# Five of nine small tiles one place earlier, and three routing groups regrouped and re-timed, in an attention and expert kernel

## The chip, the cores and the metric

The kernel runs on one core of one Trainium2 chip. The metric is the device time of one launch in microseconds (us). Three runs of the kernel before gave 518.86, 519.31 and 521.41 us; their median is 519.31 us.

A core has a matrix engine (TensorE, PE in the profile), a vector engine (VectorE, DVE), a scalar engine (ScalarE, ACT), a general engine (GpSimd, POOL) and a sync engine (SyncE, SP) that here only starts transfers. Each takes its own instructions strictly in the order in which the program emitted them, and they meet through semaphores.

## The reference

Eight batches, each with eight heads, 512 tokens and 32 states, of width 64 a head. The first part lets tokens attend to states and states to tokens; its results are put together to 8 x 544 rows of 512. The second part sends each row to one of eight experts.

```
a = softmax(scale * x @ state.T);      xread = a @ state
a2 = softmax(scale * state @ x.T);     sread = a2 @ x
x = concat([xread, sread])             # (8, 544, 512) after the heads are put side by side
logits = x @ w_gate;  local = sigmoid(x @ w_local)
for each batch, for s in 0..543:
    e = argmax(logits[s]) if s == 0 or local[s] < 0.5 else the expert of row s-1
    out[s] = softmax(logits[s])[e] * (relu(x[s] @ w1[e]) @ w2[e])
```

The expert of a row thus depends on the rows ahead of it in its batch. `w1` is 512 x 1024 and `w2` 1024 x 512 for each expert, all in 32-bit floating point.

## The kernel before

**Units.** The 512 token rows of a batch form a unit, eight in all, and each unit is computed with one expert: that of the batch's first row. Rows for which that isn't the right expert are marked as still to do (in the profiled execution no work for such rows appears). A unit has four passes (`seven`, line 987): `first_half` for two halves of the hidden layer and `second_half` for two halves of the rows. Each pass is one level of Strassen's method (seven products where eight would be the plain way), so a unit has 28 products, and all units 224. A product is four matmul statements of 128 x 128 by 128 x 256, which the profile shows as 8 matmuls. The sums of weights that Strassen's method wants are made on VectorE: `second_sum` (four additions of 128 x 1024 for `w2`), `first_sum` (four for the next unit's `w1`) and `column_sum` (four smaller ones for the next unit's rows).

**Ticks.** After each product `seven` calls `tick()`, which counts and emits whatever was registered for that product with `at(tick, ...)`; product n of the whole run is followed by tick n. So the order of the instructions on every engine is written out by hand: a step that is registered for tick 8 stands behind product 8 on TensorE, and on VectorE behind what product 8 itself left there. Within one tick the order is that of registration: sums first, then the attention of later batches (`FLOW`, products 2 to 101), then the steps of the routing groups, then the turning of a tile's rows. `second_sum` i stands at 28u + 8 + i in unit u, `column_sum` at 28u + 18 + i, `first_sum` at 28u + 22 + i. Inside `seven` the first product goes to a bank of PSUM and ScalarE copies it into the common bank (line 994), on which the third product then accumulates.

**Routing groups.** `choose` (line 555) finds the experts of a group of batches in seven steps, parted by `yield`. 1: VectorE, maxima and comparisons (lines 571 to 578). 2: ScalarE, an exponential (581). 3: TensorE, transposes into a bank (586, 587). 4: VectorE, a comparison and a scan over 544 rows (591 to 596). 5: TensorE, transposes back into another bank (602 to 604). 6: VectorE, reads that bank and writes the tokens' places (607 to 614). 7: VectorE, the probabilities (619 to 624). `GROUPS` holds the batches of each group and the seven ticks. The two banks come from a pool of three that the attention uses too.

**Tiles.** The 32 states of each batch have rows too, which can go to any expert. `route` places the 256 rows in nine tiles of 32 rows, each with one expert, 4 MB of weights. A tile has `begin` (start the load of `at`, its `w1`, 2 MB, and gather its rows), `turned` (VectorE turns the rows, three ticks before `one`), `one` (32 matmul records, line 962, then Relu and a turn), `load(1)` (start the load of `ct`, its `w2`, 2 MB) and `two` (64 records, line 975, a scaling, and a scatter of the rows by GpSimd, line 984). There are two buffers `at` and one `ct`. A tile runs between two passes: the passes are counted as places 0 to 31 (place 4u + n is pass n of unit u), `ONES` names the place behind which tile i's `one` stands, and its `two` stands behind the next place. In `bound` (line 1129) the order at one place is: `two` of the earlier tile, start of the next tile's `ct`, `one` of the own tile, start of the `at` of the tile after next. Behind the second place of a unit SyncE's queue takes the next unit's rows x and its `w1`; at the start of a unit it takes that unit's `w2`. 

**Scatters.** The rows of a unit leave in four scatters (line 1037), y0 and y1 of each of two halves. The scatters all write the same output, so one waits for the landing of the one before it, except those of the very last half, which are declared free of each other (`apart`); a tile's scatter is not in that exemption. Results of a place are handed to the next pass as `waiting`: its first entry is emitted behind that pass's third product, its others behind the product that makes the seventh sum. At the very end what is left is emitted at once: y1 of the last half, then tile 8's rows.

```
        def bound(at, behind):
            if at in twos:
                behind.append(twos[at].two())
                if twos[at].i + 1 < NTILE:
                    tiles[twos[at].i + 1].load(1)
            if at in ones:
                ones[at].one()
                if ones[at].i + 2 < NTILE:
                    tiles[ones[at].i + 2].begin()
```

Of the kernel before, what the change touches and what calls it, by code (L numbers as in the profile page):

```python
# [158 lines left out]
"""  # L159
FIRST, PERIOD = 2, 14  # L160
PER = 28
GROUPS = {(0, 2): (6, 7, 8, 9, 12, 13, 14), (2, 5): (59, 60, 61, 62, 65, 67, 68), (5, 8): (102, 103, 105, 106, 108, 110, 111)}
ONES = 18, 20, 21, 23, 24, 26, 27, 29, 30


class Attention:
# [73 lines left out]
    def do(self, name, *at):  # L240
        steps = dict(xt=self.load_t, xn=self.load_n, sc=self.scores, mx=self.maximum, nb=self.scaled, tr=self.turned,
                     zh=self.halves, mo=self.over_states, sb=self.subtract, ex=self.exponents, zs=self.sums,
                     zi=self.inverses, ml=self.shares, tb=self.turn_back, et=self.exponents_over_tokens, tu=self.turn,
                     ec=self.turned_to, iv=self.invert, sr=self.state_reads, st=self.states_to, rt=self.states_turned,
                     ws=self.states_to_rows, sl=self.state_logits, sk=self.state_logits_kept, lg=self.logits,
                     lt=self.logits_turned, vv=self.token_reads, xr=self.reads_kept, xd=self.reads_kept_too,
                     wr=self.reads_out, ga=self.gates, gl=self.gates_kept, kp=self.keep, fe=self.first_expert)
        steps[name](*at)
# [220 lines left out]
class Routing:  # L469
# [85 lines left out]
    def choose(self, bank, b0, b1):  # L555
# [34 lines left out]
        hold, run = self.hold[:n], self.ran[:n]  # L590
        nc.vector.tensor_scalar(hold, seq, 0.0, None, Alu.is_equal)
        nc.vector.tensor_tensor_scan(run, hold, seq, 0.0, Alu.mult, Alu.add)
        zp = flat(self.zp)
        nc.vector.tensor_reduce(zp, pr, axis=AX, op=Alu.add)
# [212 lines left out]
class Experts:  # L807
# [72 lines left out]
    def at(self, tick, do, *args):  # L880
        self.todo.setdefault(tick, []).append(lambda: do(*args))
# [10 lines left out]
    def run(self, start):  # L892
# [232 lines left out]

        ones = dict(zip(ONES, tiles))
        twos = {at + 1: tile for at, tile in ones.items()}
# [40 lines left out]
        at = self.at  # L1168
        for u in range(B):
            for i in range(4):  # L1170
                at(PER * u + 8 + i, self.second_sum, i)
                if u + 1 < B:
                    at(PER * u + 18 + i, self.column_sum, i)
                    at(PER * u + 22 + i, self.first_sum, i)
# [3 lines left out]
        at(2, start.zero_row)  # L1178
        for (b0, b1), ticks in GROUPS.items():
            self.steps(route.choose(start.bank, b0, b1), *ticks)  # L1180
        tick = max(max(t) for t in GROUPS.values()) + 1
        at(tick, tiles_begin)
# [101 lines left out]
```

## Time and profile before

| what | us |
|---|---|
| median of three runs | 519.31 |
| the profiled execution, its own time | 520.96 |
| span of the profiled execution, first to last instruction | 518.8 |
| TensorE busy in the span | 498.9 (96%) |
| VectorE busy | 280.7 (54%) |
| ScalarE busy | 161.1 (31%) |
| GpSimd busy | 109.8 (21%) |
| mean granted clock of TensorE | 0.983 |

The profile is one execution. A row of its timeline has the start, the duration, the engine, the line, the operation with the tiles that it writes and reads, their shapes, and in brackets how long the engine was idle ahead of it and what ended that. "PEld" is the loading of a matmul's fixed operand, which runs beside the matmuls. A table of windows gives, for each stretch, its length, the busy time of each engine with its number of instructions, then the granted clock of TensorE (1.00 is full), the share of the transfer engines and GB/s. In a table of waits a row has the total, the number of times and the longest.

### The profile page before, as it was taken

What the parts mean: (1) busy time and instruction counts of PE and PEld (TensorE: products, weight loads), DVE (VectorE), ACT (ScalarE), POOL (GpSimd) and SP (SyncE); (2) the same over time, 40 slices, a digit from 0 to 9 for tenths busy, and PEclk for the clock granted to TensorE, in tenths of its full rate; (3) what the DMA queues carried; (4) which work ended last, traced back from release to release, by engine and by line L of the source; (5) the groups of instructions that cost most, each with busy time, mean ns of one, the idle gap of its engine ahead of it and who ended that gap; (6) DMA issues with size and microseconds to landing.
All of it is one profiled execution on the core that took longest, in us unless ns stands there. A gap on an engine that the chain in (4) does not pass through costs nothing. (4 is left out here: it accounts for less than half of the span.)

```text
span 518.8 us, 10089 instructions
## 1 busy us (share of the span) xinstructions
PE 498.9 (96%) x4008; PEld 393.5 (76%) x4008; DVE 280.7 (54%) x543; ACT 161.1 (31%) x334; POOL 109.8 (21%) x134
## 2 busy tenths in 40 slices
PE   9898999999999999999999999999999999999990
PEld 3466887777877668787888888888888888888880
DVE  5878776497645976536566745073153525164110
ACT  2533425254343522434212322232123322223110
POOL 6602132322322211330021202120021202210021
PEclk9998999999999989999999999999999999999995
DMA  8994382927548164351726975674969988691230
GB/s 312 343 338 157 118 316 103 312 78 262 232 151 321 42 221 172 112 195 44 284 101 185 406 292 209 256 277 152 402 239 358 344 310 310 253 411 43 82 143 32
DMA packets 38288, 115.67 MB, mean 223 GB/s; under 512 B 7748, under 2 KB 7880, under 8 KB 34008
## 3 DMA queue, kind: packets, MB, share of 16 engines
q1 hardware_dynamic: 34952, 105.37, 56.1%
q0 software_dynamic: 3136, 9.51, 4.7%
q8 instruction: 33, 0.54, 0.4%
q14 instruction: 23, 0.19, 0.1%
q10 hardware_dynamic: 144, 0.07, 0.1%
HBM read 97.10 MB, written 17.89 MB: 222 GB/s over the span
## 5 line engine op out<-in xcount | busy, mean ns | idle before, releaser
L1053 PE MATMUL ps<-x,a 128*128 128x256 f32 x384 | 94.0, 388 | 0.1
L1053 PE MATMUL sum<-xs,a 128*128 128x256 f32 x384 | 91.7, 382 | 0.0
L1037 POOL DMA_INDIRECT out_dram<-y,tok x32 | 37.5, 1173 | 242.9 <-DVE xs L851 60.2
L1053 PEld LDWEIGHTS ps<-x,a 128*128 128x128 f32 x384 | 72.0, 191 | 14.8 <-issue 5.2
L1053 PEld LDWEIGHTS sum<-xs,a 128*128 128x128 f32 x384 | 72.6, 192 | 13.6 <-ACT s L1082 2.5
L1100 PE MATMUL ps<-c,h 128*128 128x256 f32 x264 | 63.9, 385 | 0.0
L1100 PE MATMUL ps<-c,hs 128*128 128x256 f32 x256 | 60.8, 381 | 0.0
L1100 PE MATMUL sum<-c,h 128*128 128x256 f32 x248 | 58.6, 379 | 0.0
L1100 PEld LDWEIGHTS ps<-c,h 128*128 128x128 f32 x264 | 49.0, 190 | 9.4 <-issue 2.9
L1100 PEld LDWEIGHTS ps<-c,hs 128*128 128x128 f32 x256 | 48.5, 190 | 8.9 <-issue 2.5
L1100 PEld LDWEIGHTS sum<-c,h 128*128 128x128 f32 x248 | 46.7, 190 | 6.0
L851 DVE TENSOR_TENSOR a<-a,a 128x1024 f32<-128x1024 f32 x32 | 40.2, 1294 | 2.8 <-DMA a<-in_w_dram 2.6
L851 DVE TENSOR_TENSOR c<-c,c 128x1024 f32<-128x1024 f32 x32 | 40.7, 1307 | 1.3 <-DMA c<-in_w_dram 1.0
L851 DVE TENSOR_TENSOR h<-s,s 128x512 f32<-128x512 f32 x16 | 11.1, 692 | 45.4 <-ACT s L1082 45.3
L1053 PE MATMUL ps<-xs,a 128*128 128x256 f32 x128 | 32.2, 397 | 0.1
L994 ACT COPY sum<-ps 128x512 f32<-128x512 f32 (+1 forms) x32 | 14.8, 464 | 55.6 <-PE ps L1053 27.8
L1082 ACT COPY s<-sum 128x512 f32<-128x512 f32 x32 | 18.7, 585 | 39.2 <-PE sum L1053 29.2
L1100 PE MATMUL sum<-c,hs 128*128 128x256 f32 x128 | 30.9, 384 | 0.0
L1100 PEld LDWEIGHTS sum<-c,hs 128*128 128x128 f32 x128 | 23.9, 190 | 8.0 <-issue 2.5
L1104 ACT ACTIVATE s<-sum,prob 128x256 f32<-128x256 f32 x32 | 15.1, 473 | 45.5 <-PE sum L1100 45.5
L851 DVE TENSOR_TENSOR y<-s,s 128x256 f32<-128x256 f32 x16 | 6.7, 422 | 41.4 <-ACT s L1104 41.4
L1053 PEld LDWEIGHTS ps<-xs,a 128*128 128x128 f32 x128 | 24.9, 197 | 4.6 <-DVE a L851 1.0
(186 smaller groups left out, 560.8 us busy)
## 6 DMA issues: line engine op xcount, KB each, us to landing
at<-in_w_dram SPq DMA_DIRECT2D x18, 1024.0 KB, 9.4
ct<-in_w_dram SPq DMA_DIRECT2D x18, 1024.0 KB, 9.6
a<-in_w_dram SPq DMA_DIRECT2D x32, 512.0 KB, 7.9
c<-in_w_dram SPq DMA_DIRECT2D x32, 512.0 KB, 6.9
x_t<-in_xt_dram SPq DMA_DIRECT2D x16, 512.0 KB, 6.3
x_n<-in_xn_dram SPq DMA_DIRECT2D x8, 1024.0 KB, 6.3
xts<-xr SPq DMA_DIRECT2D x28, 256.0 KB, 2.1
x<-xts SPq DMA_DIRECT2D x7, 1024.0 KB, 5.7
```

Of the source, the lines that this page charges most:

```text
L851: self.nc.vector.tensor_tensor(out, a, b, op=op)
L994: nc.scalar.copy(y, x)
L1037: put = nc.gpsimd.indirect_dma_start(out=out, out_offset=to, in_=y, in_offset=None, bounds_check=NT - 1, oob_is_err=False)
L1053: nc.tensor.matmul(to[:, m * width:m * width + width], lhsT=w[:, j, f:f + P], rhs=x[:, j, :], start=begin and m == 0 and j == 0, stop=(m = ...
L1082: return lambda t: nc.scalar.copy(to, t)
L1100: nc.tensor.matmul(to, lhsT=x[:, m, n * P:n * P + P], rhs=w[:, m, :], start=begin and m == 0, stop=(m == FK // 2 - 1), skip_group_check=True)
L1104: return lambda t: nc.scalar.activation(to, t, Act.Copy, scale=p)
```

## The change

Three tables of places are edited; no instruction is computed otherwise. The groups of batches become (0, 1), (2, 3) and (4 to 7) in place of (0, 1), (2 to 4) and (5 to 7), with new ticks. In unit 0 the third and fourth `second_sum` move from products 10 and 11 to 12 and 16. Of the nine tiles, tiles 1, 3, 5, 7 and 8 move one place earlier, and 0, 2, 4 and 6 stay: the last `one` stands behind place 29 in place of 30, and so the last `two` behind place 30, ahead of the last pass, in place of behind it.

```diff
-GROUPS = {(0, 2): (6, 7, 8, 9, 12, 13, 14), (2, 5): (59, 60, 61, 62, 65, 67, 68), (5, 8): (102, 103, 105, 106, 108, 110, 111)}
-ONES = 18, 20, 21, 23, 24, 26, 27, 29, 30
+GROUPS = {(0, 2): (6, 7, 10, 11, 13, 14, 15), (2, 4): (55, 56, 57, 59, 61, 62, 63),
+          (4, 8): (102, 103, 105, 106, 109, 110, 111)}
+ONES = 18, 19, 21, 22, 24, 25, 27, 28, 29
...
-                at(PER * u + 8 + i, self.second_sum, i)
+                at(PER * u + 8 + i if u else (8, 9, 12, 16)[i], self.second_sum, i)
```

## The prediction

> **What bounds the kernel now.** I read the page first: the shares of busy time, then the granted clock by slices.
>
> ```profile
> span 518.8 us, 10089 instructions
> ...
> PE 498.9 (96%) x4008; PEld 393.5 (76%) x4008; DVE 280.7 (54%) x543; ACT 161.1 (31%) x334; POOL 109.8 (21%) x134
> ...
> PEclk9998999999999989999999999999999999999995
> ```
>
> TensorE is busy for 96% of the span, and none of its products is removed. Time can come only from its 20 us of idleness and from stretches at a lower clock: the row PEclk has an 8 in two slices (and the 5 at the end, after the last product). So I asked what TensorE waited for, and then for its clock in windows of 3.41 us, which is how long each low stretch lasts.
>
> ```profile
> PE p L586 <- DVE top L577: 2.0, 1, 2.0
> PE p L447 <- DVE undone L611: 1.2, 1, 1.2
> ```
>
> ```profile
> core 0: us, PE busy (x) PEld busy (x) DVE busy (x) ACT busy (x) POOL busy (x), PEclk, DMA share, GB/s
> ...
> 20.09:23.51 3.42, 2.79 (x33) 1.52 (x32) 2.34 (x10) 2.14 (x6) 0.94 (x1) 1.00 0.64 193
> 43.98:47.40 3.42, 1.39 (x10) 0.82 (x9) 3.28 (x11) 0.57 (x2) 1.05 (x1) 1.00 0.89 309
> 47.40:50.81 3.41, 3.41 (x9) 2.71 (x9) 3.38 (x3) 1.00 (x4) 1.96 (x1) 0.50 0.01 5
> ...
> 180.50:183.92 3.42, 2.18 (x19) 0.82 (x18) 3.25 (x11) 1.16 (x3) 0.73 (x1) 1.00 0.16 61
> 183.92:187.34 3.42, 3.42 (x12) 2.78 (x11) 0.89 (x3) 1.59 (x3) 0.00 (x0) 0.50 0.41 148
> ```
>
> The two longest waits are in the routing groups, step 3 of the first and the bank that step 6 of the second holds. Each is in a window with 1.39 or 2.18 us of work, and the window behind each runs at clock 0.50. A full window at half clock loses 3.41 x 0.5 = 1.71 us; I call that a dip. A window with 2.79 us of work was followed by no dip. The third place is the end, shown below: TensorE is done near 505.8, 13 us ahead of the end of the span.
>
> **The change part by part.** *First group (products 6 to 15).*
>
> ```profile
> 42.78 1.89 PE L1053 MATMUL ps<-x,a 128*128 128x256 f32 x8
> ...
> 44.86 1.04 DVE L573 TENSOR_TENSOR eq<-lt,mx 128x80 f32<-128x80 f32 x1
> ...
> 46.47 0.17 DVE L577 SCALAR_TENSOR_TENSOR top<-lt,own 128x10 bf16<-128x10 f32 x1
> 46.56 0.23 DVE L578 TENSOR_TENSOR pr<-lt,mx 128x80 f32<-128x80 f32 x1
> ...
> 46.70 0.38 PE L586 MATMUL p<-identb,top 128*2 128x128 bf16 x4 [2.03 <-DVE top L577]
> ...
> 46.83 0.27 ACT L581 ACTIVATE pr<-pr 128x80 f32<-128x80 f32 x1 [3.25 <-DVE pr L578]
> 47.00 0.58 ACT L994 COPY sum<-ps 128x512 f32<-128x512 f32 x1
> ```
>
> ```profile
> 41.05 1.89 PE L1053 MATMUL sum<-xs,a 128*128 128x256 f32 x8
> ```
>
> A product takes 42.78 - 41.05 = 1.73 us from start to start. Product 8 starts at 42.78; the transposes behind it wait 2.03 us, since VectorE comes to step 1 late. Steps 1 and 2 keep their ticks, 6 and 7, so they end as now; the transposes move behind product 10. Then product 9 starts at 42.78 + 1.73 = 44.51 and its last record ends near 44.51 + 1.89 = 46.40. But product 10 accumulates on the bank that ScalarE's copy (line 994) fills, and that copy is queued behind step 2's exponential, itself held until 46.83 by step 1. The copy ends at 47.58. So the wait isn't removed but handed on: product 10 stands idle from 46.40 to some 47.64, 1.24 us in place of 2.03. The gain is 0.79. What is late next is nothing: the transposes are by then ready (46.64), step 4 stands on VectorE behind the same two sums as now, and two products still lie between step 4 and step 5. Sum 3 (tick 16) is first read by the last product of that pass, 21; sum 2 (tick 12) by product 19. If VectorE were 1 us late there, four products (6.9 us) are still ahead of the reader.
>
> Does the remaining 1.24 us of idleness still cost a dip? The row nearest to it is the second group's wait, 1.24 us too (2.18 us of work), which did. I take it that it does: 0 gained on the clock here, with 1.71 gained as the other end.
>
> By the Trainium skill ("TensorE: Matmul & The Clock Gate", Part 1, on the clock gate) the clock falls to half after at least one idle window of about 3.4 us, and windows run free of the kernel. The length agrees with the rows above (3.41 us); that a whole window must be idle does not, since windows with 1.39 and 2.18 us of work led to a dip. By that rule the remaining wait would be free of a dip, and the sum would be the rival without it.
>
> *Second group.*
>
> ```profile
> 153.84 0.43 DVE L370 TENSOR_REDUCE z<-zh 128x16 f32<-128x272 f32 x1 [2.29 <-POOL zh L367]
> ...
> 175.05 6.13 DVE L851 TENSOR_TENSOR c<-c,c 128x1024 f32<-128x1024 f32 x4
> ...
> 182.24 1.08 PE L447 MATMUL p<-a,states_of 32*32 32x512 f32 x14 [1.24 <-DVE undone L611]
> ```
>
> Now step 6 stands behind four sums (6.13 us) and holds a bank of PSUM that the token reads want. At products 55 to 63 no sum runs: the first step falls into VectorE's idle 2.29 us ahead of 153.84 (in the first group it took some 2.2 us to 46.79, with a slow 1.04 in it), and the bank is free well before the reads behind product 65. Two batches in place of three make no step longer. Gain: 1.24 us of wait and its dip of 1.71. If the cover were gone (VectorE full at 151 to 154), step 3 behind product 57 would wait, at most by the 2.03 us of group one.
>
> *Third group, four batches for three.*
>
> ```profile
> L578 DVE TENSOR_TENSOR pr<-lt,mx 128x120 f32<-128x120 f32 x2 | 0.5, 273 | 0.0
> ```
>
> One batch more cost 273 - 230 = 43 ns on this operation; over some 20 operations that is 0.9 us of VectorE, spread over ten products, where TensorE waits for none of them now. I take nothing; the ends are 0 and 0.9.
>
> *Tiles.* Their matmuls and loads are the same in number, so TensorE's work is unchanged. What can go wrong is that weights come late, since a `ct` now must land between neighbouring places five times in place of four, and 36 MB come in one place less. The tightest burst:
>
> ```profile
> 356.12 1.77 SPq L953 DMA_DIRECT2D ct<-in_w_dram  x2
> ...
> 360.24 0.79 SPq L844 DMA_DIRECT2D x<-xts  x1
> ...
> 416.23 1.32 SPq L953 DMA_DIRECT2D ct<-in_w_dram  x2
> 417.68 0.35 SPq L844 DMA_DIRECT2D x<-xts  x1
> ```
>
> ```profile
> 370.88 1.95 PE L975 MATMUL ps<-ct,htt 128*32 128x128 f32 x64
> ...
> 429.25 1.93 PE L962 MATMUL ps<-at,xtt 128*32 128x256 f32 x32
> ```
>
> ```profile
> 373.70 0.69 DVE L851 TENSOR_TENSOR xs<-x 128x512 f32<-128x512 f32 x1 [14.11 <-DMA x<-xts]
> ...
> 377.59 4.76 DVE L851 TENSOR_TENSOR a<-a,a 128x1024 f32<-128x1024 f32 x4 [0.28 <-DMA a<-in_w_dram]
> ...
> 426.62 0.69 DVE L851 TENSOR_TENSOR xs<-x 128x512 f32<-128x512 f32 x1 [9.16 <-DMA x<-xts]
> 427.23 0.30 DVE L944 STREAM_TRANSPOSE xtt<-xgt 128x128 f32<-128x128 f32 x1
> ```
>
> ```profile
> DMA to landing us min/median/max: 7.8/9.6/11.4
> ```
>
> A `ct` has 370.88 - 356.12 = 14.8 us between its issue and its `two`, and landed in 11.4 at most: 3.4 us to spare. The new pairs behind places 19, 22 and 25 have the same distance. The burst of 7 MB that is at 356 now comes at 416 (`ct`, `at`, x, `w1`), with the same places behind it. Tile 3's turning moves to tick 158, behind a `column_sum` that waits for x; tile 5 stands like that now, x landing 426.62 - 417.68 = 8.94 us after its issue, the turn done at 427.53 and `one` at 429.25, 1.7 us to spare. In the new place x follows an `at` of the same size and a `two` (1.79 us, below) stands ahead of that `one`, so it has no less. GpSimd's gathers go two places ahead of their turns. Cost: nothing.
>
> *The end.*
>
> ```profile
> 501.80 0.98 POOL L1037 DMA_INDIRECT out_dram<-y,tok  x1 [7.64 <-DVE y L1112]
> ...
> 503.82 1.95 PE L975 MATMUL ps<-ct,htt 128*32 128x128 f32 x64
> ...
> 503.93 0.48 DVE L1118 SCALAR_TENSOR_TENSOR y<-ps,prob,s 128x256 f32<-128x256 f32 x1 [0.79 <-PE ps L1100]
> 505.07 0.98 POOL L984 DMA_INDIRECT out_dram<-yt,row  x1 [2.30 <-DMA out_dram<-y,tok]
> ...
> 509.73 0.98 POOL L1037 DMA_INDIRECT out_dram<-y,tok  x1 [3.67 <-DVEq L1245]
> 513.41 0.98 POOL L984 DMA_INDIRECT out_dram<-yt,row  x1 [2.71 <-DMA out_dram<-y,tok]
> ```
>
> Four scatters leave one after the other: y0, tile 7, y1, tile 8. Tile 7's rows were ready long before, but were emitted behind y0. With the last `two` ahead of the last pass, tile 7 leaves in the pass before, and y0, tile 8, y1 remain. The last pass starts later by the `two` that now precedes it, 1.79 us: its 1.95, less the 0.16 by which a product's 1.89 exceeds its 1.73 from start to start. One tile's link, 509.73 - 505.07 = 4.66, is gone. y1 is ready at 504.41 + 1.79 = 506.20, ahead of its turn, which comes 3.27 (505.07 - 501.80) and 4.66 after y0 at 503.59, at 511.52. So the chain and not the product sets the end: 4.66 - 1.79 = 2.87 us gained. Were y0's link (3.27) the one saved, it would be 1.48; I take 2.87, since a tile's scatter is what goes.
>
> *Sum*, against the profiled execution's own 520.96 (2.16 more than its span): 520.96 - 0.79 - 1.24 - 1.71 - 2.87 = 514.3. The median of the runs, 519.31, is 1.65 below the profiled one, about one dip; the runs 518.86 and 521.41 stand as far apart as one with one dip and one with two. From 519.31 without the second dip the sum is 519.31 - 0.79 - 1.24 - 2.87 = 514.4.
>
> **Rivals.**
> *No dip.* The 1.24 us in the first group split over two windows, each with over 2.79 us of work, or are too short. Windows last 3.41, so a wait of 1.24 lies whole in one for 2.17 / 3.41 = 64% of starts. Time: 514.3 - 1.71 = 512.6.
> *No wait at all in the first group*, if ScalarE's copy gets ahead: 512.6 - 1.24 = 511.4. Against it: the copy's place behind the exponential.
> *The end doesn't shrink* (the change doesn't do there what it says): y1's last landing takes what a tile's did. Then 514.3 + 2.87 = 517.2. For it: all links are inferred from one execution.
> *Tile 3's rows late.* x landed 13.5 us after its issue behind 4 MB (360.24 to 373.70); as late here, `one` would wait 2.2 us and a dip: 518.2.
> *Slower: transfers that stand together share the rings evenly.* Then a `ct` lands with the last of its burst. 7 MB took 377.59 - 356.12 = 21.5 us, 3.07 a MB; 6 MB behind place 19 take 18.4, 3.6 over the 14.8 there are, and 7 MB behind place 25 6.7 over: 10.3 us and two dips (3.4), 528.0. It decides once a `ct` takes over 14.8 us. Against: in that very burst `two` at 370.88 followed on time, and 11.4 was the longest.
>
> **How the numbers follow.** The forecast 514.3 gets 0.47, no dip 0.28 (the 64 to 36 above), no wait 0.07, the end as before 0.10, tile 3 late 0.04, slower 0.04. A measurement tells this kernel from no change at about 0.5%, 2.6 us: faster means below 516.7. That holds the first three, 0.82; the end and tile 3 give no change, 0.14; the last slower, 0.04. The range goes from 511.4 to 517.2, widened on each side by the 0.4 between two runs with as many dips (518.86, 519.31): 511.0 to 517.6.
>
> **What would show it.** Right: the wait of the transposes gone, and a wait of about 1.2 us ahead of product 10 that ends with ScalarE's copy; no wait of the token reads near 182; at most one slice with an 8 in PEclk; three scatters behind the last pass's fifth product, the last of them y1. Wrong: a wait of line 975 or 962 on a transfer, a last scatter by line 984, or a new wait near products 57 to 61.

## The result, and the profile after

The changed kernel takes 512.40 us, the median of six runs (511.51 to 512.61), against 519.54 us for the kernel before, also six runs (518.86 to 521.41). The ratio is 0.9852, with a 95% interval of 0.9832 to 0.9873 (the quotient of the two medians is 0.9863; gains given below as "by the ratio" are worked out from the ratio and can be some tenths larger than the difference of the medians). The forecast was 514.3 in a range of 511.0 to 517.6: right in direction and within the range, and 1.9 us too slow. It came out next to the rival "no dip" (512.6). The profiled execution took 511.91 us, with a span of 510.1.

From the page of the changed kernel, the span, the busy shares and the granted clock in 40 slices:

```profile
span 510.1 us, 10091 instructions
...
PE 494.8 (97%) x4008; PEld 390.4 (77%) x4008; DVE 282.0 (55%) x543; ACT 161.0 (32%) x334; POOL 111.6 (22%) x134
...
PEclk9999999999999999999999999999999999999997
```

TensorE is busy for 4.1 us less, with the same 4008 matmuls (the two windows at half clock are gone), and no slice but the last shows a clock below 9. The lines of the changed kernel's file lie one further down than those of before (994 is now 995). TensorE's longest wait in the profile of the changed kernel:

```profile
PE sum L1054 <- ACT sum L995: 1.2, 1, 1.2
```

This is the wait that the prediction put ahead of product 10. The starts of the products, from the timelines of both kernels, show where the time went:

| stretch | before | after | change |
|---|---|---|---|
| start of the span to product 8 | 42.78 | 43.23 | +0.45 |
| product 8 to product 15 | 18.15 | 15.87 | -2.28 |
| product 15 to product 57 | 92.74 | 92.70 | -0.04 |
| product 57 to product 71 | 36.16 | 32.33 | -3.83 |
| product 71 to the last pass's scatter of y0 | 311.97 | 313.72 | +1.75 |
| scatter of y0 to the end of the span | 17.0 | 12.25 | -4.75 |

The sum is 8.7 us, the difference of the spans (518.8 - 510.1). Three places carry it, the three that the prediction named. The other stretches, but for the one that took in a tile's `two`, differ by less than 0.5 us.

*First group.* TensorE's and ScalarE's timelines of the changed kernel:

```profile
43.23 1.89 PE L1054 MATMUL ps<-x,a 128*128 128x256 f32 x8
44.96 1.89 PE L1054 MATMUL ps<-xs,a 128*128 128x256 f32 x8
48.09 1.99 PE L1054 MATMUL sum<-xs,a 128*128 128x256 f32 x8 [1.24 <-ACT sum L995]
50.01 0.38 PE L587 MATMUL p<-identb,top 128*2 128x128 bf16 x4
```

```profile
47.28 0.27 ACT L582 ACTIVATE pr<-pr 128x80 f32<-128x80 f32 x1 [3.25 <-DVE pr L579]
47.45 0.58 ACT L995 COPY sum<-ps 128x512 f32<-128x512 f32 x1
```

The wait of the transposes is gone (they start with no idle time ahead of them), and product 10 waits 1.24 us for the copy behind the exponential, to the hundredth what was worked out. But the windows of the clock around it, in the changed kernel, are all at 1.00:

```profile
43.93:47.34 3.41, 2.92 (x14) 2.23 (x12) 3.27 (x10) 0.16 (x2) 1.05 (x1) 1.00 0.90 307
47.34:50.75 3.41, 2.66 (x14) 2.01 (x15) 3.38 (x4) 3.13 (x8) 1.96 (x1) 1.00 0.03 10
50.75:54.16 3.41, 3.41 (x19) 3.03 (x18) 3.31 (x7) 1.12 (x3) 0.51 (x1) 1.00 0.01 2
```

*Second group.* The token reads behind product 68, first in the timeline of the kernel before, then of the changed one:

```profile
179.96 1.04 PE L447 MATMUL p<-a,states_of 32*32 32x512 f32 x2
...
183.26 3.16 PE L1053 MATMUL ps<-x,a 128*128 128x256 f32 x8
```

```profile
178.22 1.09 PE L448 MATMUL p<-a,states_of 32*32 32x512 f32 x16
179.23 1.99 PE L1054 MATMUL ps<-x,a 128*128 128x256 f32 x8
```

The sixteen reads now need 179.23 - 178.22 = 1.01 us until the next product starts; before they needed 183.26 - 179.96 = 3.30. The wait was thus 2.29 us, and not the 1.24 of its row.

*The end.* GpSimd's timeline of the changed kernel:

```profile
497.85 0.98 POOL L1038 DMA_INDIRECT out_dram<-y,tok  x1 [5.86 <-DVE y L1113]
501.21 0.98 POOL L985 DMA_INDIRECT out_dram<-yt,row  x1 [2.39 <-DMA out_dram<-y,tok]
504.53 0.98 POOL L1038 DMA_INDIRECT out_dram<-y,tok  x1 [2.35 <-issue]
```

Three scatters behind the last sums, y0, tile 8 and y1, where there were four.

*Tiles.* From product 71 to the scatter of y0 the stretch is longer by 1.75 us, which is the `two` that moved into it (1.79 forecast), and by nothing else. Tile 3, with its turn behind the sum that waits for x (VectorE), and its `one` (TensorE), in the changed kernel:

```profile
363.70 0.69 DVE L852 TENSOR_TENSOR xs<-x 128x512 f32<-128x512 f32 x1 [9.82 <-DMA x<-xts]
364.31 0.31 DVE L945 STREAM_TRANSPOSE xtt<-xgt 128x128 f32<-128x128 f32 x1
```

```profile
366.94 1.91 PE L963 MATMUL ps<-at,xtt 128*32 128x256 f32 x32
```

The turn ends at 364.62, 2.3 us ahead of the product (the prediction: no less than 1.7).

### The profile page after: what moved, and what is told of

The parts are those of the page before. It is cut to its first block, busy times and chain, and to the rows that moved or that the text cites. A ratio compares the mean times of both kernels' runs of the same rounds, so it can differ in the third digit from the quotient of the medians.

```text
span 510.1 us, 10091 instructions
## 1 busy us (share of the span) xinstructions
PE 494.8 (97%) x4008; PEld 390.4 (77%) x4008; DVE 282.0 (55%) x543; ACT 161.0 (32%) x334; POOL 111.6 (22%) x134
## 5 line engine op out<-in xcount | busy, mean ns | idle before, releaser
L1054 PE MATMUL ps<-x,a 128*128 128x256 f32 x384 | 92.8, 384 | 0.0
L1054 PE MATMUL ps<-xs,a 128*128 128x256 f32 x128 | 30.7, 382 | 0.5 <-DVE a L852 0.5
```

Source lines behind the costliest of these rows:

```text
L1054: nc.tensor.matmul(to[:, m * width:m * width + width], lhsT=w[:, j, f:f + P], rhs=x[:, j, :], start=begin and m == 0 and j == 0, stop=(m = ...
```

## The experiments

Each run stands beside runs of the kernel before on the same chip. The chips differ (the median of before was 519.73 us on the first, 523.60 on the second, 523.18 on the third), so times are compared within a chip, and ratios across them.

### The three parts one by one

On the kernel before, the tiles alone:

```diff
-ONES = 18, 20, 21, 23, 24, 26, 27, 29, 30
+ONES = 18, 19, 21, 22, 24, 25, 27, 28, 29
```

> The kernel before with the new places of the tiles alone. Theory (one link of the chain of scatters goes, the last pass starts one 'two' later): 4.66 - 1.79 = 2.9 us less than before, some 516.7 against 519.5, three scatters behind the last pass's fifth product, both waits of the routing groups and their dips of the clock as before, and no wait of line 962 or 975 on a transfer. Rival (the end doesn't shrink, the last landing takes its place): within 0.5 us of before. Rival (weights late in the denser places): slower than 516.7, with waits on transfers in the stretch of the tiles.

Measured: 517.28 us, ratio 0.9941 (0.9917 to 0.9964), which is 3.1 us less by the ratio (2.4 by the medians); 2.9 was expected. GpSimd's end is that of the changed kernel:

```profile
503.45 0.98 POOL L1037 DMA_INDIRECT out_dram<-y,tok  x1 [5.86 <-DVE y L1112]
506.77 0.98 POOL L984 DMA_INDIRECT out_dram<-yt,row  x1 [2.33 <-DMA out_dram<-y,tok]
510.26 0.98 POOL L1037 DMA_INDIRECT out_dram<-y,tok  x1 [2.52 <-issue]
```

Both waits of the groups are there at 2.0 and 1.2 us, each with half clock in the window behind it. No matmul of a tile waits for a transfer; the only row in which TensorE does is 0.2 us in the first attention, which the changed kernel has too. The rivals on the end and on late weights fall.

The first group and its sums alone:

```diff
-GROUPS = {(0, 2): (6, 7, 8, 9, 12, 13, 14), ...
+GROUPS = {(0, 2): (6, 7, 10, 11, 13, 14, 15), ...
...
-                at(PER * u + 8 + i, self.second_sum, i)
+                at(PER * u + 8 + i if u else (8, 9, 12, 16)[i], self.second_sum, i)
```

> The kernel before with the new ticks of the first routing group and the two moved sums of unit 0 alone. Theory of the prediction (the wait goes from 2.03 to 1.24 us and keeps its dip): 0.8 us less, 518.7. Rival (a wait of 1.24 us amid dense products costs no dip): 0.8 + 1.7 = 2.5 us less, 517.0, and full clock in the window behind product 10.

Measured: 518.28 us, ratio 0.9964 (0.9944 to 0.9985), 1.9 us less by the ratio (1.5 by the medians), between the two. The time can't decide; the windows of its profile do:

```profile
43.89:47.30 3.41, 2.21 (x11) 1.60 (x9) 3.27 (x10) 0.77 (x3) 1.05 (x1) 1.00 0.78 282
47.30:50.71 3.41, 3.37 (x18) 2.64 (x19) 3.38 (x3) 2.44 (x6) 1.96 (x1) 1.00 0.01 2
177.01:180.42 3.41, 2.17 (x18) 0.34 (x16) 3.27 (x9) 1.59 (x3) 1.18 (x2) 1.00 0.21 77
180.42:183.83 3.41, 3.41 (x14) 2.52 (x8) 0.93 (x3) 1.59 (x3) 0.00 (x0) 0.50 0.14 50
```

Here nearly all of the 1.24 us ahead of product 10 lies in one window (2.21 us of work), and the window behind it runs at full clock. The second group's wait, still in this kernel, is in a window that seems to hold as much work, 2.17 us, and is followed by half clock. So the two waits of "1.24 us" aren't alike.

The second and third group alone:

```diff
-... (2, 5): (59, 60, 61, 62, 65, 67, 68), (5, 8): (102, 103, 105, 106, 108, 110, 111)}
+... (2, 4): (55, 56, 57, 59, 61, 62, 63), (4, 8): (102, 103, 105, 106, 109, 110, 111)}
```

> The kernel before with the second and third routing group regrouped and re-timed alone. Theory of the prediction: the wait of 1.24 us and one dip of 1.71 go, 2.95 us less, 516.6. Rival (the row of that wait understates it, since two token reads had been issued and counted as work): the stretch from product 57 to 71 shrinks by 3.8 us as between the two kernels, 515.7; where the run before had no dip there, less by 1.7 in both.

Measured: 517.82 us, ratio 0.9957 (0.9937 to 0.9977), 2.2 us less by the ratio (1.9 by the medians), which is less than the 2.95 and the 3.8 expected and near the 1.7 for a run before without that dip. In its profile, products 57 to 71 take 185.20 - 152.87 = 32.33 us, as in the changed kernel. The first group is as before here, with its wait of 2.03 us, and yet the product behind it runs at full clock:

```profile
43.71 1.89 PE L1054 MATMUL ps<-x,a 128*128 128x256 f32 x8
47.63 0.38 PE L587 MATMUL p<-identb,top 128*2 128x128 bf16 x4 [2.03 <-DVE top L578]
...
48.05 1.99 PE L1054 MATMUL ps<-xs,a 128*128 128x256 f32 x8
```

```profile
43.11:46.52 3.41, 2.49 (x12) 1.86 (x10) 3.34 (x7) 0.60 (x1) 0.84 (x1) 1.00 0.70 195
46.52:49.94 3.42, 2.31 (x14) 1.96 (x15) 3.32 (x8) 1.46 (x4) 1.15 (x2) 1.00 0.41 154
49.94:53.35 3.41, 3.41 (x18) 2.95 (x17) 3.34 (x4) 1.85 (x4) 1.02 (x1) 1.00 0.01 2
```

The wait lies across two windows, some 0.9 and 1.1 us in each. In this execution products 8 to 15 take 60.18 - 43.71 = 16.47 us, against 18.15 with the dip: the dip costs 1.68. The same wait of the first group thus costs a dip in some executions (the profiles of the kernel before and of the tiles alone) and none in another, by where the windows fall. The second group's wait was followed by half clock in all three profiles that have it. By the ratio the three parts come to 3.1 + 1.9 + 2.2 = 7.2 us against 7.7 for the whole change; each part is uncertain by 1.0 to 1.2 us, so they agree, but no closer than that. The two profiled spans differ by more, 8.7 us; the one before had both dips. That the medians fall short of the expectations because only some executions have the dips is likely and not shown: the record doesn't place the half clock of the executions that weren't profiled. Their mean clock does differ: of fifteen runs of the kernel before on that chip the shortest, 518.47 us, had 0.992 and the longest, 521.84 us, 0.980.

### What makes a dip

The changed kernel with ten pauses of TensorE among the dense products of units 4 to 7; the results of the pauses aren't used:

```diff
+    def pause(self, bank, widths):
+        nc, scratch = self.nc, self.route.eq.rearrange("p b i e -> p (b i e)")
+        t, back = bank(P, SQ), bank(SQ, SQ)
+        nc.tensor.matmul(t, lhsT=self.route.ident, rhs=self.route.ident[:, :SQ], start=True, stop=True)
+        nc.vector.tensor_copy(scratch[:, :SQ], t)
+        for w in widths:
+            nc.vector.tensor_scalar(scratch[:, :w], scratch[:, :w], 1.0, None, Alu.mult)
+        nc.tensor.matmul(back, lhsT=scratch[:, :SQ], rhs=self.route.ident[:, :SQ], start=True, stop=True)
```

> The changed kernel with ten pauses of TensorE in units 4 to 7, where it otherwise never waits: a small product, a chain of VectorE copies of graded length (0 to some 2.5 us) on what it gives, and a product on the last copy; the sums of these do not enter the output. Each pause is to be about 0.6 us and its copies, 0.5 to 3 us, amid dense products. Theory of the prediction: a pause of 1.24 us that lies whole in one window of 3.41 costs a dip. Rival, after the first runs (1.21 us whole in a window gave none; the wait of the token reads was really 2.3 us): dips only where a window holds well over 1.3 us of idleness, some 1.5 to 2. Rival by the Trainium skill (TensorE: Matmul & The Clock Gate, Part 1): no dip at any pause below a whole window of about 3.4 us.

> As the run of pauses before it, with the lengths dealt to other places, so that other lengths fall whole into a window. The theories expect the same bounds as there: a dip from 1.24 us on; a dip only from 1.5 to 2 us on; none below 3.4 us.

> The changed kernel with ten pauses of TensorE of some 1.8 to 3.2 us in units 4 to 7, as in the two earlier runs of pauses, where the longest that lay whole in a window was 1.46 us and gave no dip. If a window is judged by its own idleness, with a bound between 1.46 and 2.03 us: half clock in the window behind each window that holds 2.03 us or more, and in none that holds under 1.46. If a whole idle window is needed: no dip but perhaps behind the longest.

Measured (531.39, 531.74 and 554.08 us, longer by the pauses): in the first two, with pauses of 0.28 to 1.82 us of idleness, no pause led to a dip. Two windows of the second, each with a whole pause (1.46 and 1.33 us), and what follows the first of them:

```profile
491.42:494.83 3.41, 1.95 (x12) 1.65 (x10) 1.62 (x5) 0.74 (x2) 0.00 (x0) 1.00 1.02 422
494.83:498.25 3.42, 3.42 (x18) 3.03 (x17) 0.00 (x0) 0.47 (x1) 0.00 (x0) 1.00 0.19 71
361.71:365.12 3.41, 2.08 (x13) 1.78 (x12) 1.49 (x5) 0.43 (x2) 0.00 (x0) 1.00 0.68 189
```

In the third, with pauses of 1.73 to 3.27 us:

```profile
298.41:301.83 3.42, 1.62 (x9) 1.45 (x10) 2.89 (x8) 0.29 (x1) 0.00 (x0) 1.00 0.94 332
301.83:305.24 3.41, 3.41 (x18) 3.00 (x17) 0.00 (x0) 0.95 (x2) 0.00 (x0) 1.00 0.89 346
332.55:335.96 3.41, 1.23 (x9) 1.03 (x8) 1.83 (x6) 0.58 (x1) 0.00 (x0) 1.00 0.96 384
335.96:339.37 3.41, 3.41 (x9) 2.70 (x9) 0.00 (x0) 0.00 (x0) 0.99 (x1) 0.50 1.05 402
...
404.23:407.64 3.41, 1.55 (x8) 1.38 (x9) 1.86 (x6) 0.25 (x1) 0.00 (x0) 1.00 0.95 375
407.64:411.05 3.41, 3.41 (x9) 2.71 (x9) 0.00 (x0) 0.59 (x1) 0.98 (x1) 0.50 1.02 400
411.05:414.47 3.42, 1.69 (x10) 1.39 (x9) 1.50 (x5) 0.60 (x1) 0.00 (x0) 1.00 0.61 246
```

The windows with 0.86, 1.23, 1.40, 1.52, 1.55 and 1.69 us of work were each followed by half clock; in units 4 to 7 of the three runs, those with 1.60, 1.62 and 1.70 and all above were not. A pause of 2.90 us that two windows shared (2.33 and 1.60 us of work) gave no dip, one of 1.73 us whole in a window (1.69) did. So among dense products a window is judged by its own work, and the bound is near half of it, between 1.5 and 1.7 us of 3.41. It is no sharper than that: the 1.69, which stands directly behind a window at half clock, had a dip and the 1.60 and 1.62 had none. The prediction's theory (1.24 us of idleness) falls, and so does the rule that a whole idle window is needed, which the prediction cited from the Trainium skill ("TensorE: Matmul & The Clock Gate", Part 1). Before the runs I had set the bound at 1.5 to 2 us of idleness; 1.7 to 1.9 fits.

The second group's wait can fit it too. Two token reads stand in the profile with 1.04 us of work, but sixteen of them take 1.01 when nothing holds them, so two are some 0.13; the rest was waiting. In the window 177.01 to 180.42 above, that leaves 2.17 - 0.91 = 1.26 us of work, below the bound; in the same window of the kernel before, of which 0.50 us of those reads fall inside, 2.18 - 0.50 = 1.68, at it. This correction is worked out, not measured by itself. A rival stays open: that the narrow reads (32 x 32) in those windows count for less than their time.

### The wait that is left, and the end

The changed kernel with one tick altered:

```diff
-GROUPS = {(0, 2): (6, 7, 10, 11, 13, 14, 15), ...
+GROUPS = {(0, 2): (6, 8, 10, 11, 13, 14, 15), ...
```

> The changed kernel with the first group's exponential at tick 8 in place of 7, so that ScalarE's copy into the common bank stands ahead of it. Theory (the remaining wait of product 10 is that copy queued behind the exponential): the wait goes, 1.24 us less than the changed kernel, some 511.2, and 1.7 more in executions where that wait had cost a dip. Rival (VectorE's first step or something else holds product 10): the wait stays and the time is that of the changed kernel, 512.4.

Measured: 510.78 us, ratio 0.9827 (0.981 to 0.9843), on the first chip. Its ScalarE and TensorE:

```profile
45.53 0.57 ACT L995 COPY sum<-ps 128x512 f32<-128x512 f32 x1 [1.19 <-PE ps L1054]
...
47.60 0.27 ACT L582 ACTIVATE pr<-pr 128x80 f32<-128x80 f32 x1 [0.80 <-DVE pr L579]
```

```profile
45.28 1.89 PE L1054 MATMUL ps<-xs,a 128*128 128x256 f32 x8
47.01 1.89 PE L1054 MATMUL sum<-xs,a 128*128 128x256 f32 x8
```

The copy stands ahead of the exponential, product 10 follows product 9 after 1.73 us, and products 8 to 15 take 57.92 - 43.55 = 14.37 us in place of 15.87, 1.50 less, of which 1.24 is the wait. The wait was that copy. The time alone wouldn't show it: the interval overlaps that of the changed kernel (0.9832 to 0.9873), which didn't run beside it.

The changed kernel with tile 8's scatter emitted three products earlier in the last pass:

```diff
-            for results in waiting[:1]:
+            for results in waiting if apart else waiting[:1]:
                 results()
...
                 three(y)
-                for results in waiting[1:]:
-                    results()
                 whole(4, None)
```

> The changed kernel with tile 8's scatter emitted behind the third product of the last pass, together with the scatter that already stands there, in place of behind the sixth. Its rows are ready at 488.06 in the profile of the changed kernel. Theory (the end is set by the chain y0, tile 8, y1, not by the last product): y1 leaves when its rows are ready, 500.45 in place of 504.53, so 4.1 us less than the changed kernel, some 508.3. Rival (the landing of the last scatter or the end of the program sets the end whatever is ahead of it, or the tile's scatter now delays y0): within 0.5 us of the changed kernel's 512.4.

Measured, on the second chip: 510.98 us, ratio 0.9744 (0.969 to 0.9799). And with both edits:

> The changed kernel with both edits, the exponential at tick 8 and tile 8's scatter behind the third product. If the two gains are free of each other: 510.8 - 4.1 = 506.7. If the end is not the chain: 510.8.

Measured, there too: 511.34 us, ratio 0.9755 (0.9702 to 0.9809). The intervals overlap almost wholly, so this pair doesn't tell whether the gains add. In the profile with both edits, y1 does leave 2.89 us behind y0 and product 10 doesn't wait, but TensorE waits 1.1 us for a transfer in the first attention, and two windows, from 20.91 to 27.74, run at half clock. Once more, beside the changed kernel on a third chip:

> The changed kernel once more, beside the two runs that follow, on the same chip. Theory: 1.3 to 1.5% less than before, no dip behind the wait of product 10 in the profile, whatever the phase of the windows.

> The changed kernel with tile 8's scatter behind the third product of the last pass, again, since the chip of its first run was some 4 us slower for every kernel. Theory (the chain sets the end; y1 left 2.9 us behind y0 there in place of 6.7): 3.4 to 3.8 us less than the changed kernel beside it. Rival (the end of the program doesn't follow): within 0.5 us of it.

> Both edits, again. If the two gains add: 1.2 us less than the run with the scatter alone, 4.6 to 5 less than the changed kernel. If the wait of product 10 is made up later: as the run with the scatter alone.

| kernel, third chip | median us | ratio to before (523.18) | interval |
|---|---|---|---|
| the change | 514.52 | 0.9839 | 0.9802 to 0.9876 |
| and tile 8's scatter earlier | 511.51 | 0.9789 | 0.9754 to 0.9825 |
| and the exponential later | 509.54 | 0.9746 | 0.9709 to 0.9782 |

Neighbouring intervals overlap. The runs themselves don't: 513.67 to 515.01, 510.45 to 513.12 and 509.12 to 509.75. The change is 1.6% faster here, a little more than the 1.3 to 1.5% expected.

In the profile of the change on this chip the whole wait of product 10 lies in one window, and full clock follows. So it is in four more profiles that have this wait whole in a window (the three with pauses and this chip's with the scatter earlier, 2.17 or 2.18 us of work), and in the one on the second chip with the scatter earlier:

```profile
45.61:49.03 3.42, 2.18 (x11) 1.60 (x10) 3.32 (x8) 1.67 (x5) 1.14 (x2) 1.00 0.42 155
49.03:52.44 3.41, 3.41 (x20) 2.60 (x19) 3.34 (x4) 1.53 (x4) 1.53 (x1) 1.00 0.01 2
```

GpSimd's end in the last of the three:

```profile
495.54 0.98 POOL L985 DMA_INDIRECT out_dram<-yt,row  x1 [2.53 <-DMA out_dram<-y,tok]
498.86 0.98 POOL L1036 DMA_INDIRECT out_dram<-y,tok  x1 [2.34 <-DVE y L1111]
501.75 0.98 POOL L1036 DMA_INDIRECT out_dram<-y,tok  x1 [1.91 <-DVE y L1117]
```

y1 now leaves 2.89 us behind y0 and as soon as its rows are made, where it left 6.68 behind y0 in the changed kernel (504.53 - 497.85). From the start of the last product to the end of the span the changed kernel takes 512.8 - 500.63 = 12.2 us on this chip, with the scatter earlier 509.4 - 501.00 = 8.4, so the end is 3.8 us shorter, and y0 isn't held up: it leaves 0.8 us behind its rows in both. The median falls by 3.0 us with the scatter, a little under the 3.4 to 3.8 expected (why is open), and by 2.0 more with the exponential, a little over the 1.2. Not all of the 2.0 need be the wait, since one of the two profiles has a dip near 22 us and the other none. Both edits together beat the change by 5.0 us there, and the kernel before by 2.5%.

## Why the prediction was right, and where it was off

*Right: three places.* The waits it built on, and the clock behind them, are where the time went, and the tiles cost nothing beyond the `two` that moved (the stretch grew by 1.75 against 1.79). The sizes were partly off: against the profiled execution the sum took off 6.6 us, and the spans differ by 8.7. The first group gave 1.49 more than forecast, the second 0.88, the end 0.13, and the rest of the kernel 0.41 less.

*First group, the wait.* Forecast: 2.03 becomes 1.24, a gain of 0.79, by the copy behind the exponential. Measured: exactly 1.24; the gain without dips is 16.47 - 15.87 = 0.60. The later tick of the exponential shows that the cause is as said.

*First group, the dip: the step that failed.* "I take it that it does" put 1.7 us too much into the forecast, which is nearly all of the 1.9 us between 514.3 and 512.4. The step leaned on the second group's row as nearest, 1.24 us and followed by a dip. That row was not what it seemed: TensorE counted as busy while two issued reads stood still, and the wait was 2.29 us. With dense products around it, 1.24 us leaves 2.2 us of work in a window, above the bound of 1.5 to 1.7. The rival "no dip" had the right time. Of its two reasons, the wait split over two windows held in the profile of the changed kernel (2.92 and 2.66 us of work, though not "each over 2.79") and was not needed: in the run of the first group alone the wait lay nearly whole in one window. The other, "or are too short", is the one that the runs bear out.

*Second group.* Forecast 1.24 + 1.71 = 2.95; measured 3.83 in the profiled pair, since the wait was 2.29 (the remainder, 1.54, is the dip, by difference). Run by itself the part is worth 2.2 by the ratio, less than either; why is open, since all three profiles with this wait show its dip.

*Third group.* Forecast nothing. No wait appears there; its price alone wasn't measured.

*The end.* Forecast 4.66 - 1.79 = 2.87; measured 4.75 - 1.75 = 3.00 between the profiles and 3.1 by itself. That the two are so close is luck. The prediction's own chain has the last scatter leave at 511.52, only 513.41 - 511.52 = 1.89 us earlier than before, since with 3.27 and 4.66 kept the link that goes is the 3.68 from y1 to tile 8; for 2.87 the time from the last scatter to the end would have to shrink by 1 us, and it grew from 5.4 to 5.6. What made up for it is that the link from the tile to y1 is 3.32 us here, not 4.66. Why it was longer before is not known; its row names a releaser (DVEq) that the rows after don't have. Only the number of links was understood.

*A rival's price.* The 2.2 us for tile 3's rows coming late can't be worked out from the rows beside it (13.46 - 8.94 - 1.7 would be 2.8). The rival fell all the same, with 2.3 us to spare.

*The base.* The forecast from the profiled 520.96 and that from the median 519.31 agreed at 514.3 and 514.4 only since both kept one dip. The six runs of the changed kernel lie within 1.1 us, those of the kernel before within 2.6. With both further edits, where neither group's wait is left and the profile has no dip ahead of the end, five runs on the third chip lie within 0.7 us, where the kernel before spread over 5.6. This fits waits that dip in some executions only.

## What to carry to other kernels

Among dense products a wait of the matrix engine cost its length here and, if it left a 3.4 us window of the clock less than about half full, 1.7 us more; it is worth splitting or shortening such waits even where they can't be removed. An idle row can understate a wait when a few instructions had been issued ahead of it, as in the second group: compare the stretch with the same instructions where nothing holds them. When steps are moved clear of one queue, look at the next instruction that stands behind them on every other engine, and at the end of the program count the transfers that follow one another, and emit early those whose data is ready.

## What the runs showed that was not expected

The bound of the dip among dense products is near half of a window's work, not a whole idle window, as the pauses show. Near 20 to 27 us, where narrow matmuls of the attention run, some executions of the same kernel have a dip and others none: the changed kernel's first profile has none there, its profile on the third chip has one. Three windows of the latter, one after the other:

```profile
14.89:18.31 3.42, 2.18 (x82) 1.43 (x81) 3.08 (x8) 1.94 (x5) 3.42 (x6) 1.00 1.01 417
18.31:21.72 3.41, 3.01 (x44) 0.82 (x40) 2.72 (x10) 2.66 (x7) 1.23 (x2) 1.00 0.75 308
21.72:25.13 3.41, 3.19 (x27) 2.29 (x31) 2.24 (x9) 1.34 (x3) 2.06 (x2) 0.50 0.91 285
```

The window with 2.18 us of recorded work is followed by full clock, the one with 3.01 by half. In other runs windows with 2.5 to 3.0 us were followed by half clock, and in three of them a second window at half clock came behind one with 3.27 us of work. The bound among dense products doesn't explain this; whether the records overstate the work or narrow matmuls count less stays open.
